# Attention and soft mixture of experts on one core: the output in three column groups instead of two halves, with a new order of stores and weight loads

## The chip, the core and the metric

The program runs on one core of a Trainium2 chip. The core has a matrix engine (PE, whose weight loads are shown apart as PEld), a vector engine (DVE), a scalar engine (ACT), GpSimd (POOL) and a sync engine (SP). In this kernel SP issues every transfer between the chip's main memory (HBM) and the on-chip memory, and sixteen DMA engines carry them out. Matrix products land in PSUM, the PE's accumulator memory, from which DVE or ACT copies a result to the on-chip memory.

The metric is the device time of one execution in microseconds (us). Before the change it is 398.29 us, the median of three runs (398.01 to 398.84).

## What is computed

Attention with a sigmoid in place of the softmax, for 8 batches of 12 heads, 448 tokens and 64 columns per head. Its output, as 3584 rows of 768 columns, goes through a soft mixture of 8 experts with 4 slots each:

```python
scores = scale * np.matmul(q, k.transpose(0, 1, 3, 2)) - np.log(S)
attn = 1.0 / (1.0 + np.exp(-scores))
x = (attn @ v)                                  # 3584 x 768
...
logits = x @ phi                                # 3584 x 32
d = softmax of logits over the rows;  slot_input = d.T @ x
for e in range(E):
    h = np.maximum(slot_input[e] @ w1[e], 0.0)  # 4 x 1024
    slot_out[e] = h @ w2[e]                     # 4 x 768
c = softmax of logits over the columns
return c @ slot_out                             # 3584 x 768
```

The weights are large beside the work: `w1` and `w2` hold 25.2 MB each, and the output 11.0 MB, all in float32.

## The kernel before

The program has three stages. The first is the attention, up to about 290 us, in which the rows of `x`, the logits and the running slot inputs are made. The second multiplies the slot inputs by `w1` (`w1_part`, line 518, and `h_part`, line 535), expert by expert, up to about 327 us. The third, which the change is about, multiplies by `w2` and makes the output.

Weights come in units: 128 partitions of 768 float32 columns, 384 KB, 3072 bytes to a partition, 64 units for `w1` and then 64 for `w2`. `load_unit` (line 92) puts the next unit into the next slot of a ring of 68 (`wa0` to `wa48`, `wb0` to `wb18`) and has SP issue its DMA. Output tiles take slots of the same ring in turn. SP runs its DMAs strictly in the order of the program, and a DMA whose slot or data is not ready holds all behind it. 49 units are loaded in the course of the attention, 19 right after it, and the others in `load_more`, two at a time, which stops `N_LATE` = 16 units before the end.

The third stage computes the output in two halves of 384 columns. For a half, sixteen steps (`w2_step`, line 583, one for each expert and each half of its 1024 hidden columns) accumulate into one PSUM tile, `po`; a step has four matmuls, side by side in four column groups of the array, and reads two units. `gather` (line 589) copies `po` to the on-chip memory, `sum_groups` (lines 594 and 596) adds the four partial sums with one matmul and a copy, giving `st`. Then `out_batch` (lines 561 and 566) multiplies `st` by the combine weights of one batch, four matmuls into two `px` tiles of a pool of three, and copies the two tiles out, one on ACT (128 partitions) and one on DVE (96 partitions). Each copy becomes one store, so that a batch has a pair of stores (line 574), of 384 KB and 288 KB.

The second half's steps and the first half's output are interwoven. After step 1 of the second half comes `sum_groups` of the first, and from step 3 on each step is followed by one `out_batch` of the first half. With each of the first four of these (`N_MIX`) the program puts the pair of stores and four of the 16 late units into SP's queue. After each of the steps 10 to 13 it adds three matmuls whose result is not used (`warm`, line 578). After the last step come the stores of the first half that are left, then `sum_groups` of the second half and its eight batches with their stores:

```python
    for i in range(2 * E):
        w2_step(po, 1, *divmod(i, 2))
        if i == 1:
            st = sum_groups(so)
        if 3 <= i < 3 + B:
            out_batch(0, i - 3, st)
            if i < 3 + N_MIX:
                store(2)
                for _ in range(N_LATE // N_MIX):
                    load_unit()
```

Of the kernel before, what the change touches and what calls it, by code (L numbers as in the profile page):

```python
# [9 lines left out]
F32 = mybir.dt.float32  # L10
# [6 lines left out]
B, H, S, D = 8, 12, 448, 64  # L17
DM, NSLOT, E, SPE, F = 768, 32, 8, 4, 1024
P = 128
# [3 lines left out]
NQ = NPR // 2  # L23
NKC = DM // P
NFC = F // P
HALF = DM // 2
UNIT = 768
N_A = 49
N_B = 19
N_LATE = 16  # L30
N_MIX = 4
NATT = 5
QW = 2 * S
NP = B * NPR
# [6 lines left out]
TOK = (128, 128, 96, 96)  # L41
# [6 lines left out]
def soft_moe_attention(ctx: ExitStack, tc: tile.TileContext, qk, v, phi, w1, w2, cst, out):  # L48
    nc = tc.nc
# [7 lines left out]
    ident = csb[:, 0:128]  # L57
    rep = csb[:, 128:256]
# [4 lines left out]
    lt_all = cpool.tile([P, B, P], F32, name="lt_all")  # L63
# [6 lines left out]
    nc.gpsimd.memset(lt_all, NEG)  # L70

    units = [("w1", e, 2 * uu + y, kh) for e in range(E) for uu in range(2) for kh in range(2) for y in range(2)]
    units += [("w2", hf, e, g, y) for hf in range(2) for e in range(E) for g in range(2) for y in range(2)]
    state = {"next": 0, "ring": 0, "wpb": None}
    utile = {}

    def ring_tile(dt=F32):
        n = state["ring"]
        state["ring"] = n + 1
        n %= N_A + N_B  # L80
        if n < N_A:
            return wpa.tile([P, UNIT], dt, name=f"wa{n}")
        return state["wpb"].tile([P, UNIT], dt, name=f"wb{n - N_A}")

    def load_unit():
        n = state["next"]
        if n >= len(units):
            return
        state["next"] = n + 1
        u = units[n]  # L90
        t = ring_tile()[:]
        nc.sync.dma_start(t, w1[u[1:]] if u[0] == "w1" else w2[u[1:]])
        utile[u] = t
# [22 lines left out]
    with ExitStack() as actx:  # L116
# [216 lines left out]
        def last_job(b, lg):  # L333
# [153 lines left out]
    sb2 = ctx.enter_context(tc.tile_pool(name="sb2", bufs=1, reuse_waits="tile"))  # L487
    hT = []
# [11 lines left out]
    ps_o = ctx.enter_context(tc.tile_pool(name="ps_o", bufs=2, space=PSUM, reuse_waits="tile"))  # L500

    def px_tile():
        return ps_x.tile([P, 2, 512], F32, name="px")

    def load_more():
        if state["next"] < len(units) - N_LATE:
            load_unit()

    for _ in range(N_B):
# [2 lines left out]
    def w1_part(e):  # L512
        ph = px_tile()
        for uu in range(2):
            for k2 in range(NKC // 2):
                for j in range(4):
                    kh, kc = divmod(2 * k2 + j % 2, 3)
                    nc.tensor.matmul(  # L518
                        ph[32 * j:32 * j + 32, uu, 0:256], sT[:, 3 * kh + kc, :],
                        utile[("w1", e, 2 * uu + j // 2, kh)][:, kc * 256:(kc + 1) * 256],  # L520
                        start=(k2 == 0), stop=(k2 == NKC // 2 - 1))
# [32 lines left out]
            combine_d(B - 1, sb2.tile([P, P], F32, name="tmp")[:])  # L554
    h_part(*prev)

    def out_batch(hf, b, st):
        pf = [px_tile() for _ in range(2)]
        for j in range(4):
            r = slice(32 * j, 32 * j + 32)  # L560
            nc.tensor.matmul(  # L561
                pf[j // 2][0:TOK[j], j % 2, 0:HALF], lt_all[r, b, 0:TOK[j]], st[r, :], start=True, stop=True)
        for g in range(2):
            n = TOK[2 * g]
            ov = ring_tile()[0:n, :].rearrange("p (j c) -> p j c", j=2)
            (nc.scalar.copy if g == 0 else nc.vector.tensor_copy)(ov, pf[g][0:n, :, 0:HALF])  # L566
            r0 = b * S + TOF[2 * g]
            stores.append((out[r0:r0 + 2 * n, hf * HALF:(hf + 1) * HALF].rearrange("(j p) c -> p j c", p=n), ov))

    stores = deque()  # L570

    def store(n):
        for _ in range(min(n, len(stores))):
            nc.sync.dma_start(*stores.popleft())

    def warm(n):
        for _ in range(n):
            nc.tensor.matmul(wt[:, 0:P], ident, ident, start=True, stop=True)

    def w2_step(po, hf, e, g):  # L580
        for fl in range(4):
            ut = utile[("w2", hf, e, g, fl // 2)][:, fl % 2 * HALF:(fl % 2 + 1) * HALF]
            nc.tensor.matmul(  # L583
                po[32 * fl:32 * fl + 32, 0:HALF], hT[e][:, 4 * g + fl, :], ut,
                start=(e == 0 and g == 0), stop=(e == E - 1 and g == 1))

    def gather(po):
        so = sb2.tile([P, HALF], F32, name="tmp")
        nc.scalar.copy(so[:], po[:, 0:HALF])
        return so  # L590

    def sum_groups(so):
        pr = px_tile()[:, 0, :]
        nc.tensor.matmul(pr[:, 0:HALF], rep, so[:], start=True, stop=True)
        st = sb2.tile([P, HALF], F32, name="st", bufs=2)
        nc.vector.tensor_copy(st[:], pr[:, 0:HALF])  # L596
        return st

    po = ps_o.tile([P, 512], F32, name="po")
    for e in range(E):  # L600
        for g in range(2):
            w2_step(po, 0, e, g)
            load_more()
            load_more()
    so = gather(po)
    po = ps_o.tile([P, 512], F32, name="po")
    wt = ps_o.tile([P, 512], F32, name="po")
    for i in range(2 * E):
        w2_step(po, 1, *divmod(i, 2))
        if i == 1:  # L610
            st = sum_groups(so)
        if 3 <= i < 3 + B:
            out_batch(0, i - 3, st)
            if i < 3 + N_MIX:
                store(2)
                for _ in range(N_LATE // N_MIX):
                    load_unit()
        if 2 + B <= i < 2 * E - 2:
            warm(3)
    so = gather(po)  # L620
    store(len(stores))
    st = sum_groups(so)
    for b in range(B):
        out_batch(1, b, st)
        store(2)


# [33 lines left out]
```

## Time and profile before

| quantity | value |
|---|---|
| median of three runs | 398.29 us |
| the profiled execution: its own time | 401.23 us |
| its span, first to last instruction | 399.5 us |
| PE busy | 371.3 us (93%) |
| DVE busy | 228.7 us (57%) |
| ACT busy | 186.1 us (47%) |
| weights, inputs and output moved | 97.52 MB, 244 GB/s over the span |
| mean granted PE clock | 0.98 |

The share of busy time says little here, since the stages have different limits: in the attention the PE is busy without a break, and in the last hundred microseconds the DMA engines are. A stretch of the span has therefore to be read by itself, its DMA rate beside its engines' busy time. Times within the span are counted from its start.

### The profile page before, as it was taken

The numbers are of one execution on the slowest core, as the hardware profiler recorded it, in microseconds if no ns is written. First come the engines' busy times: TensorE is split into PE (matmuls) and PEld (weight loads), VectorE is DVE, ScalarE is ACT, GpSimd is POOL, SyncE is SP. The second block draws the span as 40 slices with busy tenths as digits, with TensorE's granted clock in tenths as the row PEclk, the third lists the DMA queues.
The fourth block names the chain that finished last, engine by engine and source line by source line (L and its number), as shares of the span: only waits on it lengthen the run. The fifth ranks groups of instructions, "written<-read, shape, count | busy, mean of one in ns | idle before, by whom it ended". The sixth has DMA issues, their size and how long they took to land.

```text
span 399.5 us, 9562 instructions
## 1 busy us (share of the span) xinstructions
PE 371.3 (93%) x4000; PEld 195.1 (49%) x4000; DVE 228.7 (57%) x531; ACT 186.1 (47%) x244; POOL 3.4 (1%) x13
## 2 busy tenths in 40 slices
PE   8999999999999999899999999999989989978740
PEld 6555455555545555365545556555465543223210
DVE  3566668668777766765677777677532420330340
ACT  5655666662566656265625666564530110220330
POOL 1000000000000000000000000000010000000000
PEclk9999999999999999989999999999999999999985
DMA  7556567645655755475546656632899999999996
GB/s 237 197 189 232 180 235 257 222 150 161 225 199 192 276 199 178 140 250 178 180 120 251 220 175 239 235 126 71 304 344 334 405 400 400 400 410 409 355 288 205
DMA packets 41851, 97.52 MB, mean 244 GB/s; under 512 B 4304, under 2 KB 16208, under 8 KB 41808
## 3 DMA queue, kind: packets, MB, share of 16 engines
q1 hardware_dynamic: 41808, 96.91, 69.1%
q8 instruction: 31, 0.51, 0.5%
q14 instruction: 12, 0.10, 0.1%
HBM read 85.43 MB, written 11.47 MB: 243 GB/s over the span
## 4 chain that ended last, share of the span: by engine, by line
PE 78%; DMA 12%; DVE 3%; issue 2%; SPq 1%; ACT 0%; ACTq 0%
PE b L186 25%; PE b L168 21%; PE b L195 6%; PE px L518 5%; PE b L307 4%; PE po L583 4%; PE b L179 4%; DMA wb<-in_w_dram 4%; DMA zd<-t 3%; PE b L215 3%; PE px L561 2%; DMA dr<-zd 2%; DMA wa<-in_w_dram 2%; DMA out_dram<-wa 1%; PE px L535 1%
## 5 line engine op out<-in xcount | busy, mean ns | idle before, releaser
L158 ACT ACTIVATE att<-b,nbias 128x896 f32<-128x896 f32 x144 | 132.1, 1020 | 1.3 <-PE b L168 1.1
L186 PE MATMUL b<-att,v 128*64 128x448 f32 x576 | 115.3, 545 | 0.1
L168 PE MATMUL b<-qs,ks 64*128 64x448 f32 x864 | 96.3, 373 | 0.7 <-issue 0.5
L168 PEld LDWEIGHTS b<-qs,ks 64*128 64x128 f32 x864 | 80.2, 188 | 24.8 <-PE b L195 14.8
L186 PEld LDWEIGHTS b<-att,v 128*64 128x64 f32 x576 | 38.5, 137 | 62.6 <-issue 47.4
L158 ACT ACTIVATE attm<-b,nbias 128x896 f32<-128x896 f32 x24 | 24.2, 1010 | 71.6 <-PE b L179 71.6
L147 DVE CAST qs<-qkt 128x448 fp32r<-128x448 f32 x48 | 18.8, 392 | 51.5 <-DMA qkt<-in_qk_dram 47.4
L149 DVE TENSOR_TENSOR qs<-qkt,qs 128x448 fp32r<-128x448 f32 x48 | 30.0, 626 | 1.6
L204 DVE COPY xT<-b 128x896 f32<-128x896 f32 x23 | 25.1, 1090 | 8.6 <-PE b L195 8.5
L149 DVE TENSOR_TENSOR ks<-qkt,ks 128x384 fp32r<-128x384 f32 x48 | 26.8, 558 | 1.6
L210 DVE STREAM_TRANSPOSE y<-xT 128x448 f32<-128x448 f32 x48 | 27.3, 618 | 0.4
L179 PE MATMUL b<-qkt 64*64 64x448 f32 x192 | 22.9, 538 | 2.2 <-issue 2.2
L195 PE MATMUL b<-attm,v 64*64 64x448 f32 x192 | 23.6, 562 | 0.0
L307 PE MATMUL b<-y,dr 32*32 32x192 f32 x896 | 20.0, 332 | 0.8 <-DMA dr<-zd 0.5
L566 DVE COPY wa<-px 96x768 f32<-96x768 f32 x13 | 12.2, 952 | 13.5 <-PE px L561 12.7
L518 PE MATMUL px<-wa,sT 128*32 128x256 f32 x294 | 17.8, 381 | 0.9 <-DVE sT L378 0.9
L566 ACT COPY wa<-px 128x768 f32<-128x768 f32 x13 | 10.3, 799 | 17.9 <-PE px L561 15.2
L561 PE MATMUL px<-st,lt_all 32*128 32x384 f32 (+1 forms) x128 | 16.7, 525 | 1.5 <-DVE st L596 0.7
L215 PEld LDWEIGHTS b<-xT,phit 128*32 128x32 f32 x384 | 9.1, 109 | 17.0 <-issue 11.3
L147 DVE CAST ks<-qkt 128x384 fp32r<-128x384 f32 x47 | 16.6, 353 | 0.0
L215 PE MATMUL b<-xT,phit 128*32 128x96 f32 (+1 forms) x384 | 16.0, 266 | 0.2
L307 PEld LDWEIGHTS b<-y,dr 32*32 32x32 f32 x896 | 12.8, 103 | 6.5 <-DMA dr<-zd 2.3
(132 smaller groups left out, 223.4 us busy)
## 6 DMA issues: line engine op xcount, KB each, us to landing
wa<-in_w_dram SPq DMA_DIRECT2D x96, 384.0 KB, 7.7
qkt<-in_qk_dram SPq DMA_DIRECT2D x48, 448.0 KB, 5.0
wb<-in_w_dram SPq DMA_DIRECT2D x32, 384.0 KB, 7.1
v<-in_v_dram SPq DMA_DIRECT2D x24, 448.0 KB, 3.3
out_dram<-wa SPq DMA_DIRECT2D x13, 384.0 KB, 5.8
out_dram<-wa SPq DMA_DIRECT2D x13, 288.0 KB, 5.6
dr<-zd SPq DMA_DIRECT2D x28, 64.0 KB, 2.0
out_dram<-wb SPq DMA_DIRECT2D x3, 384.0 KB, 7.3
```

The costliest lines, as they stand in the source:

```text
L147: copy(dst[:, 0, :], src)
L149: nc.vector.tensor_tensor(out=dst[:, 1, :], in0=src, in1=dst[:, 0, :].bitcast(F32), op=ALU.subtract)
L158: nc.scalar.activation(att[:], sc[:, :, 0:S], AF.Sigmoid, bias=nbias, scale=QSCALE)
L168: nc.tensor.matmul(sc[:, h, 0:S], ks[r, z, c * P:(c + 1) * P], qs[r, y, :], start=(z + y == 0), stop=(z == 1))
L179: nc.tensor.matmul(sc[r, h, 0:S], t[d, S + NQK:QW], t[d, 0:S], start=True, stop=True)
L186: nc.tensor.matmul(avs["p", p][r, 0:S], vs[n][:, i * (NFULL + 1) + c, r], atts[p, c][:, h, :], start=(start and c == 0), stop=(stop and c ...
L195: nc.tensor.matmul(avs["p", 2 * n + i][d, 0:S], vt[r, NFULL, d], att[r, h, :], start=start, stop=stop)
L204: nc.vector.tensor_copy(xTs[n][:], avs[n][:, :, 0:S])
L210: nc.vector.transpose(ys[b][:, hp, :], xTs["p", p])
L215: nc.tensor.matmul(lp[32 * j:32 * j + 32, 0:TOK[j]], phi_sb[:, p % NPR, :], xTs["p", p][:, TOF[j]:TOF[j] + TOK[j]], start=(first and m == ...
L307: nc.tensor.matmul(sl[a // 2][32 * j:32 * j + 32, a % 2, 0:NPR * BLK], drs[b][32 * a:32 * a + 32, j, c * BLK:(c + 1) * BLK], y[32 * a:32 * ...
L518: nc.tensor.matmul(ph[32 * j:32 * j + 32, uu, 0:256], sT[:, 3 * kh + kc, :], utile[("w1", e, 2 * uu + j // 2, kh)][:, kc * 256:(kc + 1) * ...
```

## The change

The output is made in three column groups of 256. A step of 256 columns reads four pieces of 256 columns, and a unit holds three such pieces, so that the 64 units of `w2` are cut anew on the host, in the order of the steps: a group takes 64 pieces, 21 1/3 units. The steps number 48 instead of 32, `gather` and `sum_groups` run three times instead of twice, and 24 `out_batch` calls instead of 16 make 48 stores of 256 KB and 192 KB instead of 32 of 384 KB and 288 KB. A row of a store goes from 1536 to 1024 bytes. The `warm` matmuls are gone.

32 units instead of 16 are now late. 16 of them stand in pairs behind the eight pairs of stores of the first group; the other 16 behind the first five pairs of the second group, as 4, 3, 3, 3 and 3.

```diff
+NCG = 3
+CG = DM // NCG
-N_LATE = 16
-N_MIX = 4
+LATE = ((2,) * B, (4, 3, 3, 3, 3))
...
     def load_more():
-        if state["next"] < len(units) - N_LATE:
+        if state["next"] < len(units) - sum(LATE[0] + LATE[1]):
             load_unit()
...
-    def w2_step(po, hf, e, g):
+    def w2_step(po, cg, e, g):
         for fl in range(4):
-            ut = utile[("w2", hf, e, g, fl // 2)][:, fl % 2 * HALF:(fl % 2 + 1) * HALF]
+            u, y = divmod((cg * E + e) * NFC + 4 * g + fl, 3)
             nc.tensor.matmul(
-                po[32 * fl:32 * fl + 32, 0:HALF], hT[e][:, 4 * g + fl, :], ut,
+                po[32 * fl:32 * fl + 32, 0:CG], hT[e][:, 4 * g + fl, :], utile["w2", u][:, y * CG:(y + 1) * CG],
                 start=(e == 0 and g == 0), stop=(e == E - 1 and g == 1))
...
+    for cg in range(NCG):
+        po = ps_o.tile([P, 512], F32, name="po")
+        for i in range(2 * E):
+            w2_step(po, cg, *divmod(i, 2))
+            if cg == 0:
+                load_more()
+                load_more()
+                continue
+            if i == 1:
+                st = sum_groups(so)
+            if 3 <= i < 3 + B:
+                b = i - 3
+                out_batch(cg - 1, b, st)
+                if b < len(LATE[cg - 1]):
+                    store(2)
+                    for _ in range(LATE[cg - 1][b]):
+                        load_unit()
+        so = gather(po)
     store(len(stores))
     st = sum_groups(so)
     for b in range(B):
-        out_batch(1, b, st)
+        out_batch(NCG - 1, b, st)
         store(2)
```

The first place is SP's queue where the first stores come. Before, the last units of `load_more` and then the first pair; the names are ring slots:

```order
L92 DMA wa38_3998<-in_w2_dram 128x768
L92 DMA wa39_4000<-in_w2_dram 128x768
L92 DMA wa40_4023<-in_w2_dram 128x768
L92 DMA wa41_4025<-in_w2_dram 128x768
L92 DMA wa42_4031<-in_w2_dram 128x768
L92 DMA wa43_4033<-in_w2_dram 128x768
L574 DMA out_0_dram<-wa44_4240 128x2x384
```

The same place in SP's queue after the change:

```order
L92 DMA wa26_3918<-in_w2_dram 128x768
L92 DMA wa27_3920<-in_w2_dram 128x768
L574 DMA out_0_dram<-wa28_4207 128x2x256
L574 DMA out_0_dram<-wa29_4209 96x2x256
L92 DMA wa30_4213<-in_w2_dram 128x768
L92 DMA wa31_4215<-in_w2_dram 128x768
L574 DMA out_0_dram<-wa32_4227 128x2x256
L574 DMA out_0_dram<-wa33_4229 96x2x256
```

The last load ahead of the first store is now that of slot 27 and no longer that of slot 43: sixteen loads that stood ahead of the first store stand behind it.

The second place is SP's queue where the stores of the first group end and those of the second begin, after the change (slots `wb9` and `wb10` hold the last two units of the first sixteen late ones):

```order
L574 DMA out_0_dram<-wb7_4347 128x2x256
L574 DMA out_0_dram<-wb8_4349 96x2x256
L92 DMA wb9_4353<-in_w2_dram 128x768
L92 DMA wb10_4355<-in_w2_dram 128x768
L574 DMA out_0_dram<-wb11_4406 128x2x256
L574 DMA out_0_dram<-wb12_4408 96x2x256
L92 DMA wb13_4412<-in_w2_dram 128x768
L92 DMA wb14_4414<-in_w2_dram 128x768
L92 DMA wb15_4416<-in_w2_dram 128x768
L92 DMA wb16_4418<-in_w2_dram 128x768
L574 DMA out_0_dram<-wb17_4430 128x2x256
```

And the PE at the same place, after the change (`px` is the tile of an `out_batch`, `po` that of the third group):

```order
L590 MATMUL px_4388<-tmp_4377,csb_66 128x256
L579 MATMUL po_4379<-wb6_4335,acc_3694 32x256 x2
L579 MATMUL po_4379<-wb9_4353,acc_3694 32x256 x3
L579 MATMUL po_4379<-wb10_4355,acc_3694 32x256 x3
L561 MATMUL px_4400<-st_4390,lt_all_70 128x256 x2
L561 MATMUL px_4401<-st_4390,lt_all_70 96x256 x2
L579 MATMUL po_4379<-wb13_4412,acc_3694 32x256 x3
L579 MATMUL po_4379<-wb14_4414,acc_3694 32x256
L561 MATMUL px_4424<-st_4390,lt_all_70 128x256 x2
L561 MATMUL px_4425<-st_4390,lt_all_70 96x256 x2
```

The pair in `wb11` and `wb12` is the copy of the first two `px` tiles here. On the PE these stand behind the matmuls that read `wb10`, and in SP's queue the load of `wb10` is the last transfer ahead of that pair. Before the change there was no second group, and the last loads and the first half's last four pairs followed each other in SP's queue without such a border.

More of the change, by code (lines that the diff above doesn't have):

```diff
@@ L25 @@
 NFC = F // P
-HALF = DM // 2
+NCG = 3
+CG = DM // NCG
 UNIT = 768
@@ L72, in soft_moe_attention @@
     units = [("w1", e, 2 * uu + y, kh) for e in range(E) for uu in range(2) for kh in range(2) for y in range(2)]
-    units += [("w2", hf, e, g, y) for hf in range(2) for e in range(E) for g in range(2) for y in range(2)]
+    units += [("w2", i) for i in range(NCG * E * NFC // 3)]
     state = {"next": 0, "ring": 0, "wpb": None}
@@ L555, in soft_moe_attention, with out_batch @@
     h_part(*prev)
-    def out_batch(hf, b, st):
+    def out_batch(cg, b, st):
         pf = [px_tile() for _ in range(2)]
@@ L561, in out_batch @@
             nc.tensor.matmul(
-                pf[j // 2][0:TOK[j], j % 2, 0:HALF], lt_all[r, b, 0:TOK[j]], st[r, :], start=True, stop=True)
+                pf[j // 2][0:TOK[j], j % 2, 0:CG], lt_all[r, b, 0:TOK[j]], st[r, :], start=True, stop=True)
         for g in range(2):
             n = TOK[2 * g]
-            ov = ring_tile()[0:n, :].rearrange("p (j c) -> p j c", j=2)
-            (nc.scalar.copy if g == 0 else nc.vector.tensor_copy)(ov, pf[g][0:n, :, 0:HALF])
+            ov = ring_tile()[0:n, 0:2 * CG].rearrange("p (j c) -> p j c", j=2)
+            (nc.scalar.copy if g == 0 else nc.vector.tensor_copy)(ov, pf[g][0:n, :, 0:CG])
             r0 = b * S + TOF[2 * g]
-            stores.append((out[r0:r0 + 2 * n, hf * HALF:(hf + 1) * HALF].rearrange("(j p) c -> p j c", p=n), ov))
+            stores.append((out[r0:r0 + 2 * n, cg * CG:(cg + 1) * CG].rearrange("(j p) c -> p j c", p=n), ov))
     stores = deque()
@@ L574, in store @@
             nc.sync.dma_start(*stores.popleft())
-    def warm(n):
-        for _ in range(n):
-            nc.tensor.matmul(wt[:, 0:P], ident, ident, start=True, stop=True)
-    def w2_step(po, hf, e, g):
+    def w2_step(po, cg, e, g):
         for fl in range(4):
-            ut = utile[("w2", hf, e, g, fl // 2)][:, fl % 2 * HALF:(fl % 2 + 1) * HALF]
+            u, y = divmod((cg * E + e) * NFC + 4 * g + fl, 3)
             nc.tensor.matmul(
-                po[32 * fl:32 * fl + 32, 0:HALF], hT[e][:, 4 * g + fl, :], ut,
+                po[32 * fl:32 * fl + 32, 0:CG], hT[e][:, 4 * g + fl, :], utile["w2", u][:, y * CG:(y + 1) * CG],
                 start=(e == 0 and g == 0), stop=(e == E - 1 and g == 1))
     def gather(po):
-        so = sb2.tile([P, HALF], F32, name="tmp")
-        nc.scalar.copy(so[:], po[:, 0:HALF])
+        so = sb2.tile([P, CG], F32, name="tmp")
+        nc.scalar.copy(so[:], po[:, 0:CG])
         return so
@@ L593, in sum_groups @@
         pr = px_tile()[:, 0, :]
-        nc.tensor.matmul(pr[:, 0:HALF], rep, so[:], start=True, stop=True)
-        st = sb2.tile([P, HALF], F32, name="st", bufs=2)
-        nc.vector.tensor_copy(st[:], pr[:, 0:HALF])
-        return st
[L599 to L620, printed above, removed]
+        nc.tensor.matmul(pr[:, 0:CG], rep, so[:], start=True, stop=True)
+        st = sb2.tile([P, CG], F32, name="st", bufs=2)
+        nc.vector.tensor_copy(st[:], pr[:, 0:CG])
+        return st
+    for cg in range(NCG):
[16 more added lines that the diff above has]
+        so = gather(po)
     store(len(stores))
@@ L642 @@
     w1 = inputs["moe_w1"].reshape(E, 2, 3, P, 4, 256).transpose(0, 4, 1, 3, 2, 5).reshape(E, 4, 2, P, UNIT)
-    w2 = inputs["moe_w2"].reshape(E, 2, 2, 2, P, 2, HALF).transpose(5, 0, 1, 3, 4, 2, 6).reshape(2, E, 2, 2, P, UNIT)
+    w2 = inputs["moe_w2"].reshape(E, 2, 2, 2, P, NCG, CG).transpose(5, 0, 1, 3, 2, 4, 6).reshape(-1, 3, P, CG)
+    w2 = w2.transpose(0, 2, 1, 3).reshape(-1, P, UNIT)
     cst = np.zeros((P, CW), np.float32)
```

## Prediction

> **What bounds the kernel now.** I read the chain of work that ended last first, then the rates by stretch, then the packets. The chain, where the third stage runs (start, duration, what):
>
> ```profile
> 345.43 7.49 DMA wa<-in_w_dram
> ...
> 356.53 7.32 DMA wb<-in_w_dram
> ...
> 363.92 7.35 DMA wb<-in_w_dram
> ```
>
> The chain goes through transfers, and the PE only takes what has landed. The stretches show it (PE, PEld, DVE, ACT and POOL busy, then the granted PE clock, the DMA engines' share and GB/s):
>
> ```profile
> 310.00:330.00 20.00, 18.79 (x284) 10.23 (x280) 6.73 (x19) 2.80 (x13) 0.00 (x0) 1.00 1.03 402
> ...
> 350.00:360.00 10.00, 7.85 (x58) 2.07 (x56) 3.08 (x4) 2.40 (x3) 0.00 (x0) 1.00 1.04 410
> 360.00:372.00 12.00, 10.27 (x68) 4.29 (x64) 0.95 (x1) 0.80 (x1) 0.00 (x0) 1.00 1.04 407
> 372.00:374.00 2.00, 1.06 (x4) 0.30 (x2) 0.27 (x1) 0.48 (x1) 0.00 (x0) 1.00 1.07 401
> ...
> 378.00:398.00 20.00, 6.20 (x40) 2.28 (x40) 5.58 (x7) 4.12 (x6) 0.00 (x0) 0.71 0.85 264
> ```
>
> From 310 to 374 us the sixteen engines are full (a share over 1, since packets overlap a little) at 401 to 410 GB/s, loads and stores alike. After 374 us only stores are left, and the rate falls to 264. So from about 310 us on the end is set by bytes over rate, plus any time in which the queue stands empty; before the change it never does until the last half's stores. What the change can win is the slow stretch: fewer bytes left for it. What it can lose is a hole in the queue, and at 400 GB/s no later stretch can make up for one.
>
> Packets of three stretches (310 to 330, 372 to 374 and 386 to 394 us), each with the share of the queue's packets in sixteen engines' time:
>
> ```profile
> q1 hardware_dynamic: 2930, 8.00, 102.4%
> ```
>
> ```profile
> q1 hardware_dynamic: 560, 0.80, 107.2%
> ```
>
> ```profile
> q1 hardware_dynamic: 1589, 2.28, 93.0%
> ```
>
> 8.00 MB of loads are 2604 packets of 3072 bytes (the rest are small marks): 1.024 x 16 x 20 / 2604 = 0.1258 us each. 0.80 MB of stores are 522 packets of 1536 bytes: 1.072 x 16 x 2 / 522 = 0.0657. In the third stretch 2.28 MB in 8 us are 286 GB/s.
>
> **The first hole.** SP's queue around the last loads ahead of the stores (start, duration):
>
> ```profile
> 325.76 0.33 SPq L92 DMA_DIRECT2D wa<-in_w_dram  x1
> ```
>
> ```profile
> 341.36 0.33 SPq L92 DMA_DIRECT2D wa<-in_w_dram  x1
> 343.90 0.90 SPq L574 DMA_DIRECT2D out_dram<-wa  x2
> ```
>
> ```profile
> v<-in_v_dram SPq DMA_DIRECT2D x24, 448.0 KB, 3.3
> ...
> wa<-in_w_dram SPq DMA_DIRECT2D x47, 384.0 KB, 7.7
> ```
>
> A load takes 0.393 MB / 0.405 = 0.97 us of the engines and 7.7 us from issue to landing, so eight are under way. Before, the last early load is issued at 341.36 and the first store 2.5 us later: the queue stays fed. The change withholds 16 more loads; counted back at 0.97 us apiece, the last early one is the load issued at 325.76, which lands at 325.76 + 7.7 = 333.5. Behind it SP holds the first store, for which group 0 has to be finished. PE, ACT and DVE rows for that:
>
> ```profile
> 305.58 2.80 PE L518 MATMUL px<-wa,sT 128*32 128x256 f32 x48
> ...
> 327.36 1.50 PE L583 MATMUL po<-wb,acc 128*32 128x384 f32 x16
> ...
> 339.11 0.91 PE L594 MATMUL px<-tmp,csb 128*128 128x384 f32 x2
> ```
>
> ```profile
> L566 DVE COPY wa<-px 96x768 f32<-96x768 f32 x8 | 7.4, 950 | 3.8 <-PE px L561 3.0 <-DMA out_dram<-wa 0.8
> ...
> L561 PE MATMUL px<-st,lt_all 32*128 32x384 f32 x32 | 7.0, 527 | 1.2 <-DVE st L596 0.7 <-DVE wa L566 0.5
> ...
> L566 ACT COPY wa<-px 128x768 f32<-128x768 f32 x8 | 6.3, 799 | 5.5 <-PE px L561 2.8 <-DMA out_dram<-wa 2.6
> ...
> L596 DVE COPY st<-px 128x384 f32<-128x384 f32 x1 | 0.6, 558 | 12.6 <-PE px L594 12.6
> L589 ACT COPY tmp<-po 128x384 f32<-128x384 f32 x1 | 0.5, 478 | 11.3 <-PE po L583 11.3
> ```
>
> A step of 256 columns has the form of line 518's matmuls (128x256 on 32 columns): 24 matmuls, six rounds of four, in 2.73 us to the next line's start, 0.455 us a step. Group 0 needs nothing but early units, so it runs from 327.36 for 16 x 0.455 = 7.3, to 334.66. Two steps of the next group (0.91, the `gather` beside them), `sum_groups` at two thirds of 0.91 less its overlap, 0.57, two more steps (0.91, the copy to `st`, 0.43, beside them), half of an `out_batch` (0.30) and ACT's copy: from 0.478 us for 384 and 0.799 for 768 elements it takes 0.59 for 512. Together 334.66 + 0.91 + 0.57 + 0.91 + 0.30 + 0.59 = 337.9, rounded to 338.0 with the waits between engines. A transfer that finds the queue empty lands its own time plus about 2.1 us after issue (3.3 us for 448 KB of `v`, of which 1.13 are transfer). So the landings resume as from 340.1 instead of 333.5: **6.6 us** without data.
>
> **The second and third hole.** Group 0's stores then run well: steps 4 to 7 need early units only, SP refills up to eight transfers, and eight pairs (1.22 us each, below) and 16 loads (0.97) take 25.3 us, until about 365. But the load in `wb10` is the last in the queue, and the next pair needs the step that reads it. Behind its landing come a step 0.46, half an `out_batch` 0.30, ACT 0.59, waits 0.05 and the 2.1 of an empty queue: 3.5 us. The step after that needs the second of the next four loads (`wb14`), behind which two loads are under way (1.94 us): another 3.5 - 1.94 = 1.5 us. From then on the loads run ahead.
>
> The clock raises both. Rows of a stretch in the attention, where the PE waited:
>
> ```profile
> 168.00:171.00 3.00, 0.83 (x13) 0.20 (x7) 3.00 (x7) 0.00 (x0) 0.00 (x0) 1.00 0.49 156
> 171.00:175.00 4.00, 4.00 (x28) 3.17 (x22) 2.11 (x4) 2.92 (x3) 0.00 (x0) 0.57 0.56 150
> ```
>
> After three microseconds with the PE 28% busy it ran for most of the next four at half clock. Between its landings the changed kernel's PE has a step and at times an `out_batch` (0.46 + 0.60) in 3.1 us, a pair and two loads: 34% busy and less, and the `warm` matmuls, which fill such waits before the change, are gone. At half clock step and half `out_batch` cost 0.76 more: holes of **4.3 and 2.3 us**. I take that. (The Trainium skill, "TensorE: Matmul & The Clock Gate", What's actually happening, has the clock fall only after a wholly idle window of about 3.4 us; by that rule a PE that does a step in every load's time keeps its full clock, and this is a rival below. The rows above, a fall after 2.2 us of waiting, speak against it.)
>
> **The last group.** Behind the last load stand three pairs of the second group, 3 x 1.22 = 3.7 us. Meanwhile the last step (0.46), `gather` 0.37, `sum_groups` 0.57, `st` 0.43, half an `out_batch` 0.30, the copy 0.59, waits 0.1 and 2.1: 4.9 us at full clock, 6.3 at half. The difference, **1.2 us** (2.6 at half clock), is a fourth hole. I take the full clock here, since the last three or four loads come without stores between them.
>
> **Packets.** No row has a packet of 1024 bytes. From the two above, 0.0391 us per 1000 bytes and 0.0056 fixed: 0.0457, an estimate. A pair then takes 28 packets an engine, 1.28 us, 1.22 with the overlap of about 5%; at 405 GB/s it would take 1.13. Ends: nothing (by bytes) and 0.0657 a packet, the 1536-byte row (0.62 a pair more). I take the estimate, 0.09 x 16 pairs ahead of the last group, less what 1536-byte stores already lose: **+1.0 us**, between 0 and +9. (By the Trainium skill, "Advanced Engine Details and Errata", Clock Domains, an unobstructed 1 KiB descriptor takes 42 to 43 ns, by which a pair would be near 1.15 us and this term +0.3.)
>
> **What it wins.** The slow stretch holds 3.67 MB instead of 5.51. At its 286 GB/s that is 12.8 us instead of 19.3, and the 1.84 MB moved ahead cost 4.5 at 405: **-1.9 us**. Here too there are two ends: if each packet, not each byte, takes the time, 3584 packets of 1024 bytes need the same 19.3 us, and the term is +4.5. At full rate (401) it would be -5.6. I take bytes; the loads above were bound by bytes at both packet sizes.
>
> **The sum.** 6.6 + 4.3 + 2.3 + 1.2 + 1.0 - 1.9 = **+13.5 us**. Copies (48 of 0.59 and 0.69 us instead of 32 of 0.80 and 0.95), the third `gather` and `sum_groups` and the PE's steps cost nothing beyond this: the PE has waits for landings beside them; without that cover the third `sum_groups` with its copies would be 1.4 us. The profiled span of 399.5 would become 413.0, its execution's 401.23 us 414.7; the median lies 2.9 below that execution, so 398.3 + 13.5 = **411.8**.
>
> **Rivals.**
> Faster: the holes stay covered. It takes the first pair ready by 331.4 us (333.5 less 2.1). Then 8.26 MB behind the last load become 5.05; before, they took from 371.3 (the last load of the chain, 363.92 + 7.35) to about 398.4, 304 GB/s; 5.05 MB take 16.6 instead of 27.1 and the moved 3.2 MB 7.9: -2.6, 395.7 us. For it: the rate in mixed stretches, 407 against 264. Against it: at 331.4 the PE would have done about 9 of the 16 steps of group 0. It decides once all holes together are under 2.6 us. Chance 0.05; another 0.03 that holes and gain cancel.
> Full clock throughout: 6.6 + 3.5 + 1.5 + 1.2 + 1.0 - 1.9 = +11.9, 410.2. Half clock also at the end: +14.9, 413.2. These belong to the forecast's family, 0.62 together.
> The slow stretch is bound by packets: +4.5 for -1.9, 418.2. For it: the drop in rate comes with stores alone. Against it: stores alone went at 401 from 372 to 374. Chance 0.15.
> Smaller holes, if an empty queue answers sooner or group 0 is faster than line 518: 403 to 408, chance 0.12. More than all this, 0.03.
>
> **Range.** 406 to 419 leaves out about 2 in 10. A measurement of this kernel tells about 0.2% from no change; slower by more than that 0.92, within it 0.03, faster 0.05.
>
> **What would show it.** In the changed profile: a stretch of several microseconds near 334 to 340 us with hardly any bytes and SP waiting for ACT's copy; two smaller ones near 365 and 373; a granted clock of 0.5 in parts of 345 to 390; the last load landing near 390 instead of 371; some 13 us of stores alone after it at 250 to 290 GB/s. I am wrong if SP issues the first store before 333 us, if the rate in the mixed stretch is far from 400, or if the stores alone run at 400.

## The result, and the profile after

The changed kernel takes **421.88 us**, the median of five runs (420.04 to 422.49); the kernel before, on the same chip, 398.44 us (398.01 to 398.89). The ratio is **1.0579**, with a 95% interval from 1.0552 to 1.0606: slower by 23.4 us. The forecast was slower, 411.8 us with a range up to 419.0. The direction held and the size did not: the time lies 10.1 us above the forecast and outside its range. The profiled execution of the changed kernel took 422.49 us with a span of 420.7, where before it was 401.23 and 399.5. Some executions of a kernel on this chip fall into a slower state; the ratios here and below leave them out and the medians keep them (so that a ratio need not be the quotient of two medians), and one trace, that of the kernel with many warm matmuls, is of such an execution.

The GB/s in the page's slices of the changed kernel (40 slices of 10.5 us; the third stage begins in the 32nd):

```profile
GB/s 230 176 203 227 199 178 245 207 158 253 215 201 164 218 192 219 219 219 151 193 242 195 164 245 132 150 165 320 315 404 400 224 235 401 315 193 272 400 190 246
```

Before, the rate stood at about 400 or more from 310 to 374 us. Now it falls in three places, to 224, 193 and 190 GB/s, with slices at 400 between them. The same by stretches of 5 us (PE, PEld, DVE, ACT and POOL busy, granted PE clock, DMA share, GB/s):

```profile
330.00:335.00 5.00, 5.00 (x100) 2.99 (x92) 0.00 (x0) 0.37 (x1) 0.00 (x0) 1.00 0.41 156
335.00:340.00 5.00, 5.00 (x66) 2.06 (x58) 1.80 (x3) 1.17 (x2) 0.00 (x0) 1.00 0.17 54
340.00:345.00 5.00, 3.39 (x42) 1.19 (x38) 2.06 (x3) 1.75 (x3) 0.00 (x0) 1.00 0.91 276
...
360.00:365.00 5.00, 3.12 (x19) 0.73 (x20) 0.00 (x0) 0.37 (x1) 0.00 (x0) 0.50 1.06 405
365.00:370.00 5.00, 4.75 (x29) 1.60 (x27) 0.56 (x2) 0.20 (x1) 0.00 (x0) 0.58 0.18 70
370.00:375.00 5.00, 0.00 (x0) 0.00 (x0) 0.55 (x1) 0.39 (x1) 0.00 (x0) 0.76 0.72 210
375.00:380.00 5.00, 4.55 (x32) 1.38 (x32) 0.69 (x1) 0.58 (x1) 0.00 (x0) 0.55 0.49 196
380.00:385.00 5.00, 2.06 (x30) 0.74 (x22) 1.37 (x2) 1.17 (x2) 0.00 (x0) 1.00 0.94 257
385.00:390.00 5.00, 4.36 (x37) 1.50 (x34) 0.82 (x2) 0.78 (x2) 0.00 (x0) 0.66 1.03 385
...
400.00:405.00 5.00, 3.68 (x20) 1.69 (x15) 0.67 (x2) 0.68 (x2) 0.00 (x0) 0.50 0.44 153
405.00:410.00 5.00, 5.00 (x36) 2.74 (x32) 2.50 (x4) 2.62 (x5) 0.00 (x0) 0.50 0.73 213
```

What each stretch loses against a full queue is 5 us x (1 - rate / 405). 330 to 345 lose 3.1 + 4.3 + 1.6 = 9.0 us, 365 to 390 lose 4.1 + 2.4 + 2.6 + 1.8 + 0.2 = 11.2, and 400 to 405 lose 3.1. In the stretches between, at 395 to 405 GB/s, next to nothing is lost. SP's queue shows why the bytes stop (start, duration, what; "x2" is a pair):

```profile
320.33 6.14 SPq L92 DMA_DIRECT2D wa<-in_w_dram  x7
338.30 1.19 SPq L574 DMA_DIRECT2D out_dram<-wa  x2
...
370.42 0.91 SPq L574 DMA_DIRECT2D out_dram<-wb  x2
371.41 1.87 SPq L92 DMA_DIRECT2D wb<-in_w_dram  x4
379.27 0.92 SPq L574 DMA_DIRECT2D out_dram<-wb  x2
...
405.30 11.52 SPq L574 DMA_DIRECT2D out_dram<-wa  x16
```

The last early load is issued at 326.1 and lands at 334.0 by the trace's transfer records; SP's next DMA is the first store, 4.3 us after that. The same happens before the stores at 370.42, 379.27 and 405.30: each is issued after the last transfer ahead of it has landed (at 367.88, 378.24 and 403.37). What SP waited for, over the third stage (us in total, times, longest us):

```profile
SPq L574 <- ACT wa L566: 20.3, 7, 11.2
SPq L574 <- ACT wb L566: 14.5, 3, 7.9
```

The same wait before the change:

```profile
SPq L574 <- ACT wa L566: 6.8, 4, 3.0
```

The chain that ended last now leaves the transfers at 399.80 (393.05 + 6.75) and ends on the PE and its copies:

```profile
371.41 4.00 DMA wb<-in_w_dram
...
375.45 2.00 PE po L579 x8
377.46 1.16 PE px L561 x6
...
393.05 6.75 DMA wa<-in_w_dram
...
399.85 1.06 PE po L579 x6
...
401.26 0.38 ACT tmp L585
...
401.69 1.23 PE px L590 x2
...
402.94 0.43 DVE st L592
...
403.42 10.84 PE px L561 x62
```

Before, the chain went from load to load up to 371.26 with the queue full. Here it also runs through steps and batches of the PE, and at 399.85 through five links before the first store of the last group can go.

### The profile page after: what moved, and what is told of

Read it like the earlier page. It is cut to its first block, busy times and chain, and to the rows that moved or that the text cites. A ratio compares the mean times of both kernels' runs of the same rounds, so it can differ in the third digit from the quotient of the medians.

```text
span 420.7 us, 9955 instructions
## 1 busy us (share of the span) xinstructions
PE 384.6 (91%) x4170; PEld 200.4 (48%) x4170; DVE 230.1 (55%) x540; ACT 187.0 (44%) x253; POOL 3.4 (1%) x13
## 4 chain that ended last, share of the span: by engine, by line
PE 82%; DMA 12%; DVE 1%; issue 1%; SPq 1%; ACT 1%; ACTq 0%
PE b L186 26%; PE b L168 21%; DMA wa<-in_w_dram 6%; PE b L195 5%; PE px L518 5%; PE po L579 5%; PE px L561 4%; PE b L179 4%; PE b L307 4%; PE b L215 3%; DMA wb<-in_w_dram 3%; DMA zd<-t 1%; PE px L535 1%; DMA v<-in_v_dram 1%; PE b L402 1%
## 5 line engine op out<-in xcount | busy, mean ns | idle before, releaser
L168 PEld LDWEIGHTS b<-qs,ks 64*128 64x128 f32 x864 | 78.5, 185 | 26.4 <-PE b L195 15.5
L561 PE MATMUL px<-st,lt_all 32*128 32x256 f32 (+1 forms) x192 | 25.0, 553 | 0.5 <-DVE st L592 0.5
L179 PE MATMUL b<-qkt 64*64 64x448 f32 x192 | 23.8, 555 | 1.9 <-issue 1.9
L566 ACT COPY wa<-px 128x512 f32<-128x512 f32 x20 | 11.7, 585 | 28.4 <-PE px L561 27.8
L566 DVE COPY wa<-px 96x512 f32<-96x512 f32 x19 | 13.0, 687 | 20.1 <-PE px L561 20.1
L579 PE MATMUL po<-wa,h 128*32 128x256 f32 x140 | 14.1, 417 | 6.9 <-DMA wa<-in_w_dram 6.9
L592 DVE COPY st<-px 128x256 f32<-128x256 f32 x3 | 1.3, 424 | 32.7 <-PE px L590 32.7
L561 PEld LDWEIGHTS px<-st,lt_all 32*128 32x128 f32 (+1 forms) x192 | 12.1, 228 | 14.5 <-issue 6.2
```

The source lines that it names most:

```text
L168: nc.tensor.matmul(sc[:, h, 0:S], ks[r, z, c * P:(c + 1) * P], qs[r, y, :], start=(z + y == 0), stop=(z == 1))
L179: nc.tensor.matmul(sc[r, h, 0:S], t[d, S + NQK:QW], t[d, 0:S], start=True, stop=True)
L561: nc.tensor.matmul(pf[j // 2][0:TOK[j], j % 2, 0:CG], lt_all[r, b, 0:TOK[j]], st[r, :], start=True, stop=True)
L579: nc.tensor.matmul(po[32 * fl:32 * fl + 32, 0:CG], hT[e][:, 4 * g + fl, :], utile["w2", u][:, y * CG:(y + 1) * CG], start=(e == 0 and g == ...
```

## The experiments

The theory after the result: the loss is the emptying of SP's queue, and an emptying costs more than the wait and a transfer's start, since the rate comes back slowly. The rivals: the smaller and more numerous stores and copies; the half clock; and the slow rate of stores alone. All edits are to the changed kernel unless the heading names the kernel before. The times scatter by about 2% between runs, most of it ahead of the third stage, whose first step starts between 326.1 and 334.2 us in the traces, so the table gives beside the ratio (to the kernel before on the same chip) four times of each trace, by its transfer records.

| kernel | late units | last early load landed | first store issued | last load landed | last store landed | ratio, 95% interval |
|---|---|---|---|---|---|---|
| before | 16 | 349.30 | 343.90 | 371.26 | 398.43 | 1 |
| the change | 32 | 334.00 | 338.30 | 399.80 | 419.70 | 1.0579 (1.0552 to 1.0606) |
| late in group 1 only | 16 | 348.60 | 341.90 | 373.19 | 396.36 | 1.0042 (0.9998 to 1.0087) |
| late in group 2 only | 16 | 347.73 | 340.94 | 385.50 | 405.01 | 1.0236 (1.0178 to 1.0294) |
| halves, 24 late | 24 | 343.55 | 346.14 | 384.14 | 409.73 | 1.0325 (1.0268 to 1.0383) |
| three groups, 24 late, fed | 24 | 343.25 | 340.00 | 381.45 | 401.70 | 1.0077 (1.0039 to 1.0115) |
| border fed | 32 | 337.97 | 344.19 | 398.16 | 416.94 | 1.0419 (1.0304 to 1.0533) |
| warm matmuls, many | 32 | 338.78 | 345.12 | 406.00 | 426.00 | 1.0612 (1.0499 to 1.0725) |
| warm matmuls, few | 32 | 334.26 | 339.66 | 400.58 | 420.04 | 1.0549 (1.0450 to 1.0647) |

### The 16 late units of the first group alone

```diff
-LATE = ((2,) * B, (4, 3, 3, 3, 3))
+LATE = ((2,) * B, ())
```

> Three column groups as changed, but only 16 late units, in pairs behind the first group's eight pairs of stores; none behind the second group's. Theory 'empty queue' (each time SP's queue runs empty costs the time until bytes land again, plus a refill at 250 to 280 GB/s): the queue never empties before the last group, since 112 units are issued ahead of the first store as before. Last load lands near 374 (32 loads of 0.97 and 8 pairs of 1.22 from 333.5), then 8 pairs 9.8, then the last group's 3.67 MB in 10 to 13 us: 394 to 398 us, faster than before. Theory 'smaller stores' (48 stores with 1024-byte rows and their copies are what costs): slower than before, 405 us or more. Theory 'clock' (the missing extra matmuls): some 3 us at the end only, 400 us.

Measured: 399.39 us, ratio 1.0042 (0.9998 to 1.0087), so no loss, but not the gain down to 394 to 398 us that was expected either. Three groups, rows of 1024 bytes, 48 stores and 48 copies are all in this kernel. Its stretches:

```profile
335.00:340.00 5.00, 5.00 (x72) 2.08 (x63) 2.24 (x4) 1.76 (x3) 0.00 (x0) 1.00 1.03 400
...
365.00:370.00 5.00, 2.66 (x26) 0.60 (x22) 0.69 (x1) 0.58 (x1) 0.00 (x0) 1.00 1.05 397
```

The first store is issued 6.7 us ahead of the last early landing, the share stays above 1 and the rate at 390 to 401 through the mixed stretch. Net of the shorter slow stretch, smaller stores and their copies thus cost 0.4% here, 0.9% at the interval's far end, and the rival that blames them for the 5.8% falls. What moving stores ahead wins at the end (23.2 us from the last load to the last store instead of 27.2) is mostly paid beforehand (the last load lands at 373.2 instead of 371.3).

### The 16 late units of the second group alone

```diff
-LATE = ((2,) * B, (4, 3, 3, 3, 3))
+LATE = ((0,) * B, (4, 3, 3, 3, 3))
```

> Three column groups, 16 late units, all behind the second group's first five pairs (4, 3, 3, 3, 3) as changed; none behind the first group's. The first and the second emptying of the queue are gone, the third (second pair of the second group) and the wait ahead of the last group stay. Theory 'empty queue': 16 loads and 8 pairs from 333.5 to 359, five pairs and 16 loads to 380, one emptying of about 4, last load at 384, the last group as in the changed kernel: 401 to 406 us. Theory 'smaller stores': still above 415 us.

Measured: 407.6 us, ratio 1.0236 (1.0178 to 1.0294). This is a little more than the 401 to 406 expected. The first hole is gone (first store 6.8 us ahead of the last early landing); the one ahead of the second group's second pair stands (this pair is issued at 364.11, 0.8 us after the last landing), with stretches of 177 GB/s (360 to 365 us) and 270 (365 to 370). Neither set of 16 late units alone costs what the two together cost (1.0042 and 1.0236 against 1.0579): only with both does the first store have no load under way ahead of it.

### The kernel before, with 24 late units

```diff
-N_LATE = 16
+N_LATE = 24
```

> The kernel before with 24 late units instead of 16 (six behind each of the first four pairs), nothing else. Its last early load lands near 341.3, the first store is issued near 343.9: the queue empties once. Theory 'empty queue': 4.7 us until bytes land again plus about 1.7 of refill, about +6.4: 404 to 406 us. Theory that only the groups' number matters: no change, 398 to 399 us.

Measured: 410.84 us, ratio 1.0325 (1.0268 to 1.0383). This kernel has the old halves, with rows of 1536 bytes. SP's queue, then its stretches:

```profile
346.14 0.91 SPq L574 DMA_DIRECT2D out_dram<-wa  x2
...
356.88 0.91 SPq L574 DMA_DIRECT2D out_dram<-wa  x2
```

```profile
340.00:345.00 5.00, 4.91 (x42) 1.31 (x34) 0.56 (x1) 0.48 (x1) 0.00 (x0) 1.00 0.42 162
345.00:350.00 5.00, 0.27 (x4) 0.00 (x0) 0.95 (x1) 0.80 (x1) 0.00 (x0) 0.73 0.57 170
350.00:355.00 5.00, 3.00 (x12) 0.88 (x16) 0.00 (x0) 0.00 (x0) 0.00 (x0) 0.50 0.98 350
355.00:360.00 5.00, 5.00 (x40) 1.15 (x32) 1.91 (x2) 1.60 (x2) 0.00 (x0) 0.75 0.67 214
360.00:365.00 5.00, 2.27 (x14) 0.75 (x16) 0.95 (x1) 0.80 (x1) 0.00 (x0) 0.94 1.00 330
```

The queue empties once and later runs down to a single transfer, and the kernel is slower with nothing of the three groups in it. The forecast of 404 to 406 us had only the first of these. The first emptying has a gap of 346.14 - 343.55 = 2.6 us and, with the 2.1 us of a transfer that finds the queue empty, should lose 4.7; the stretches from 340 to 355 lose 3.0 + 2.9 + 0.7 = 6.6. The second loses 2.4 + 0.9 = 3.3 where the wait accounts for 1.7 (the last landing is at 357.33, 0.45 us behind the issue). So each of the two costs 1.6 to 1.9 us beyond the wait and the start.

### The border between the groups fed

```diff
-LATE = ((2,) * B, (4, 3, 3, 3, 3))
+LATE = ((2, 2, 2, 2, 2, 2, 2, 6), (0, 3, 3, 3, 3))
```

> The changed kernel, with the four late units of the second group's first pair moved ahead of that pair (behind the first group's last pair: 6 instead of 2, then 0, 3, 3, 3, 3); nothing else. The first emptying (338 us) stays, the second and third should go, since 3.9 us of loads are under way while the PE, ACT and SP make the pair. Theory 'empty queue': of the 5.3 and 5.4 us lost at these two places about 8 come back: 412 to 415 us. Rival (the loss sits in packets, copies or the clock): 420 to 422.

Measured: 419.0 us, ratio 1.0419 (1.0304 to 1.0533): faster than the change, but not the 412 to 415 us expected. All 32 units are still late, but four loads of the second group stand ahead of its first pair. From the first store's issue to the last store's landing it takes 72.75 us, where the changed kernel takes 81.40: 8.65 less. The attention of this profiled execution ended 5.9 us later than that of the changed kernel (first step at 333.29 and 327.40), so the spans don't show it. The dip at the border is now one instead of two:

```profile
370.00:375.00 5.00, 5.00 (x37) 1.70 (x34) 0.64 (x2) 0.28 (x1) 0.00 (x0) 0.76 1.03 414
375.00:380.00 5.00, 4.05 (x48) 1.48 (x42) 2.53 (x4) 2.06 (x4) 0.00 (x0) 1.00 0.74 219
380.00:385.00 5.00, 1.84 (x8) 0.33 (x8) 0.00 (x0) 0.00 (x0) 0.00 (x0) 0.76 0.96 293
385.00:390.00 5.00, 5.00 (x41) 1.71 (x40) 1.37 (x2) 1.17 (x2) 0.00 (x0) 0.56 1.05 404
```

The queue never stood empty there: the next pair was issued at 375.33, 1.9 us before the last landing ahead of it. It ran down to two or three transfers, and that alone cost 2.3 + 1.4 = 3.7 us. The changed kernel loses 11.2 from 365 to 390, so that 7.5 of the 8.65 us come from the border.

### Three groups with 24 late units, fed ahead of the stores and at the border

```diff
-LATE = ((2,) * B, (4, 3, 3, 3, 3))
+LATE = ((2, 2, 2, 2, 2, 2, 2, 4), (0, 3, 3))
```

> The changed kernel with 24 late units: two behind each of the first group's first seven pairs, four behind the eighth, three behind the second and the third pair of the second group. Stores of both groups still stand between loads, but by the reckoning the queue never empties: the last early load lands near 341, the first pair is ready at 338.3, and at the border three or four loads are under way while the next pair is made. Theory 'empty queue': from the first store's issue to the end about 58 us as with 16 late units, instead of 81; 396 to 402 us. Rival (late units or stores between loads cost by themselves): 408 or more.

Measured: 402.91 us, ratio 1.0077 (1.0039 to 1.0115), with as many late units as the halves that took 1.0325.

```profile
340.00:345.00 5.00, 5.00 (x66) 1.97 (x66) 2.63 (x5) 2.25 (x4) 0.00 (x0) 1.00 0.97 311
345.00:350.00 5.00, 5.00 (x76) 2.51 (x76) 2.32 (x4) 1.86 (x4) 0.00 (x0) 1.00 1.00 340
...
365.00:370.00 5.00, 3.84 (x36) 1.29 (x38) 1.41 (x3) 1.17 (x2) 0.00 (x0) 1.00 1.04 407
...
385.00:390.00 5.00, 5.00 (x34) 3.04 (x36) 2.06 (x3) 1.77 (x4) 0.00 (x0) 0.50 0.69 215
```

The first store goes out 3.3 us ahead of the last early landing and the border is fed. What is left is a queue that has run down to four transfers at the first store (311 and 340 GB/s from 340 to 350, 2.0 us), and one that has run down to two ahead of the last group (215 GB/s, 2.3 us); from the first store to the end it takes 61.7 us, where 58 were expected. It is not the number of withheld loads that costs, but that the queue runs down.

### The clock restored

Unused matmuls in the waits of the second and third group's steps, many in the first kernel and few in the second:

```diff
+            if cg == 1 and i >= 8 or cg == 2 and i < 2 * E - 1:
+                warm(4)
```

```diff
+            if cg > 0 and 11 <= i < 2 * E - 1:
+                warm(2)
+            if cg == 2 and i == 3:
+                warm(8)
```

> The changed kernel with four extra matmuls of 128 columns after the steps in which the PE waits (steps 8 to 15 of the second group, 0 to 14 of the third), as before the change; their results are not used. Theory 'clock': the granted clock stays at 1.0 through the third stage, and the steps, sums and copies behind each emptying and the last group shorten: 415 to 418 us instead of 421.9. Theory 'empty queue' alone: the queue still empties at the same places; less than 1.5 us are won, 420.4 to 421.9.

> The changed kernel with extra matmuls only where the PE surely waits: two after each of steps 11 to 14 of the second and third groups, eight after step 3 of the third; their results are not used. Theory 'clock': the step behind the third emptying and the last group run at full clock, about 1 us at the third emptying, 1.4 us ahead of the last group's first store and up to 1 us in its copies: 418 to 420 us. Theory that the clock is beside the point: 421 to 423.

Measured: ratios 1.0612 (1.0499 to 1.0725) and 1.0549 (1.0450 to 1.0647), both as the change within their intervals, and neither faster than it, as the theory 'clock' had it. From first store to end they take 80.9 and 80.4 us, the change 81.4. With many, the clock stood at 1.00 in most stretches, but the matmuls themselves held up the steps: the last step ended 2.9 us after the last load instead of 1.1. With few, the first store of the last group followed the last load by 4.6 us instead of 5.5. The half clock is thus worth about 1 us as far as it could be taken away, and it is not the main cause. What a full clock without extra matmuls would save was not shown.

### The last stores: more of them ready, a second queue, a warm clock

Four kernels on why stores alone move slowly. The first is the kernel before with the last half's 16 stores held until all are ready, the second the kernel before with every first store of a last pair issued by ACT's queue; the third and the fourth are the kernel with late units in the first group only, once with warm matmuls and once with ACT's queue.

```diff
-            nc.sync.dma_start(*stores.popleft())
+            nc.sync.dma_start(*(stores.pop() if last else stores.popleft()))
...
-        store(2)
+    store(len(stores), last=True)
```

> The kernel before, with the last half's 16 stores issued in reverse order, so that SP waits for the last copy and then finds all 16 ready: eight under way at once. If the slow stretch of stores (264 to 286 GB/s) comes from too few stores under way, they now run at 380 to 400 GB/s: 5.5 MB in 14 us behind the last copy near 386, end near 402. If stores alone are slow by themselves, 19 us behind it: 407 or more.

```diff
-            nc.sync.dma_start(*stores.popleft())
+            (nc.scalar if both and k == 0 else nc.sync).dma_start(*stores.popleft())
...
-        store(2)
+        store(2, both=True)
```

> The kernel before; of the last half's stores the 128-partition ones are issued by ACT, the 96-partition ones by SP. If the slow stretch of stores alone (264 to 300 GB/s with four or five under way) comes from the way one queue issues them, the last 5.5 MB run at up to 400 GB/s and the end comes up to 5 us earlier: 393 to 396 us. If stores alone are slow for another reason, within 1 us of before.

```diff
+            if cg == 2 and 11 <= i < 2 * E - 1:
+                warm(2)
```

> Three groups, 16 late units behind the first group's pairs only, with two extra matmuls after each of steps 11 to 14 of the third group (results not used). If the slow stores at the end come from the last group being made at half clock (1.35 us a pair against 1.22 us that the DMA engines need), they run at 370 GB/s and the end comes 3 us earlier than without, about 396 us. If the slow rate has another cause, 398 to 400.

> Three groups with 16 late units behind the first group's pairs only, and the last group's 128-partition stores issued by ACT. If one queue's issue limits stores alone, 3 to 4 us earlier than without: 394 to 396; otherwise 398 to 400.

Measured: held until ready, 411.03 us, ratio 1.0227 (1.0121 to 1.0332); the 16 stores, issued from 387.9 on with no copy to wait for, still need 20.8 us for 5.51 MB. SP's queue, then the stretches:

```profile
387.90 16.78 SPq L574 DMA_DIRECT2D out_dram<-wa  x16
```

```profile
388.00:398.00 10.00, 0.00 (x0) 0.00 (x0) 0.00 (x0) 0.00 (x0) 0.00 (x0) 0.58 0.92 292
398.00:409.00 11.00, 0.00 (x0) 0.00 (x0) 0.00 (x0) 0.00 (x0) 0.00 (x0) 0.50 0.75 235
```

The eight stores under way that this kernel was made for did not come about. With all 16 ready, SP still took 16.78 / 16 = 1.05 us for each issue, where the pair of stores issued at 343.90 before the change took it 0.90 together, and by the transfer records three to five stores were under way at a time, as many as in the kernel before from 380 to 396 us. So it shows that waiting for copies is not what holds the stores back, and not what eight under way would do.

Two queues on the kernel before: ratio 1.0011 (0.9965 to 1.0056), 27.12 us from last load to end where the kernel before takes 27.17:

```profile
380.00:385.00 5.00, 3.88 (x28) 1.40 (x24) 2.71 (x3) 1.76 (x3) 0.00 (x0) 1.00 0.99 304
```

Warm matmuls with late units in the first group only: ratio 1.0036 (0.9983 to 1.0089). The clock is full up to 385 us and the stores are as slow:

```profile
380.00:385.00 5.00, 4.33 (x42) 2.21 (x40) 3.55 (x6) 3.18 (x6) 0.00 (x0) 1.00 0.97 301
385.00:390.00 5.00, 0.26 (x4) 0.00 (x0) 0.69 (x1) 0.13 (x1) 0.00 (x0) 0.77 0.98 302
```

Two queues on that kernel: ratio 0.9980 (0.9935 to 1.0025). Neither the readiness of the copies, nor the number of queues, nor the clock sets the rate of stores alone, and the bytes of a row make little difference: from 385 to 390 us the kernel with late units in the first group only, with 1024-byte rows, moves 297 GB/s, and the kernel before, with 1536-byte rows, 286 from 390 to 395. What does set it stays open; the number of transfers under way is a rival that no run varied by itself. No kernel of these can be told from the kernel before as faster.

## Why the prediction was wrong in size

**The first hole: place and wait right, price too low.** The first store was forecast for 338.0 and was issued at 338.30; the landing before it for 333.5, and it came at 334.0. The wait is 4.3 us, where 4.5 stood in the sum. The start was shorter than its 2.1 us: this store of 0.26 MB landed 2.30 us after its issue, and 0.65 of these are its own time at 405 GB/s. From landing to landing the hole is thus 6.0 us, not 6.6. But the stretches up to 345 lose 9.0 us, and 0.2 more up to 360, where the hole and the packets of eight pairs (0.7) were to cost 7.3. The step that failed is that the queue runs at full rate up to its last landing and resumes at full rate from the first new one: the sum has no term for the run-out and the refill, and here they are worth about 3 us. From 331 to 334 us, ahead of the last landing, the rate is 265, 95 and 12 GB/s in one microsecond after the other; from 339 to 343, with SP issuing again, it is 238. The transfers of 380 to 385 us show the refill, beside those of 350 to 360 (packets with how many are small, then the queue's share of sixteen engines' time):

```profile
DMA packets 776, 1.29 MB, mean 257 GB/s; under 512 B 59, under 2 KB 507, under 8 KB 776
...
q1 hardware_dynamic: 776, 1.29, 94.0%
```

```profile
DMA packets 2499, 4.00 MB, mean 400 GB/s; under 512 B 206, under 2 KB 1699, under 8 KB 2498
...
q1 hardware_dynamic: 2498, 3.98, 104.8%
```

With the prediction's 0.0457 us for a packet of 1024 bytes and 0.1258 for one of 3072, the second stretch should take 1493 x 0.0457 + 800 x 0.1258 = 168.9 us of engine time, and takes 1.048 x 160 = 167.7: the prediction's packet price was right for a full queue. The first should take 448 x 0.0457 + 269 x 0.1258 = 54.3, and takes 0.94 x 80 = 75.2. After an emptying the engines count as busy, and the packets take 1.38 times as long on average. This does not hold for every packet: by the trace's packet records the median is 46 ns for 1024 bytes and 121 ns for 3072 in both stretches. But from 380 to 385 us 145 of 717 packets take over 1.3 times their median, up to 1.6 us, and from 350 to 360 only 6 of 2292. Most packets are as fast as ever, and one in five stalls.

**The second and third hole: +11.2 instead of 6.6.** They stand where they were forecast in SP's queue, behind the load in `wb10` and behind the four loads after it, at half clock (0.58 and 0.55) as was assumed. Counted from landing to landing as in the prediction they are 4.1 and 2.6 us (2.5 and 1.0 of wait, then 1.5 and 1.6 of start), where 4.3 and 2.3 stood. So the waits were right, and the other 4.5 of the 11.2 us are run-out and refill again: 380 to 390 loses 2.0 us with SP already issuing. That the waits came out so close is in part luck. The start had been put too high, and half an `out_batch` too low: in the third hole the copy on ACT started only when the four matmuls of its batch were all but done, 1.16 us at half clock instead of 0.60.

**The last group: +4.0 instead of 1.2.** From the last landing, 399.80, to the first store it took 5.5 us where 2.8 stood in the sum (4.9 less the 2.1). The chain shows the links: at half clock the step took 1.06 instead of 0.46, `sum_groups` 1.23 instead of 0.57, and the batch and its copy from 403.42 to 405.27. I had taken the full clock here, since the last loads come without stores between; the row from 400 to 405 has 0.50. With the start, counted as 2.1 here and in the next paragraph, and less the 3.6 us in which the leftover pairs still moved, this hole is 4.0. The rival of half clock at the end was right as to the clock, and too low in price.

**Packets and slow stretch: right.** The 16 last stores take 405.30 to 419.70, 12.3 us behind the 2.1 of the start, for which the sum had 12.8; the rate goes by bytes, and the rival by which it goes by packets (418.2) came near the time for a reason that is not the one at work. The full-clock rival (410.2) and that of smaller holes fell with the rows above; the faster one needed the first pair by 331.4.

**From the span to the median.** The terms give 1.9 more for the first hole, 4.6 for the next two, 2.8 for the last and 0.5 less for the slow stretch: 8.8. The span rose by 21.2 instead of 13.5, so 7.7 had to be found. The rest of 1.1 lies in the kernel before: behind its last load it takes 27.2 us for 8.26 MB and loses 6.8 against 405 GB/s, where the sum had 19.3 - 13.6 = 5.7 for the slow stretch. A further 2.3 us is no matter of the kernel: I had put the median 2.9 us below the profiled execution, as it lay before, but that of the changed kernel lies 0.6 below.

What of this was shown: that the emptied queue is the cause, by the three kernels that keep it fed and by the halves that empty it; that the price of an emptying is more than wait and start, by two kernels with different rows. Why some packets stall after an emptying was not tried and stays open.

The clock is half again in stretches in which the PE is busy for a good part: 0.50 from 360 to 365 us, with 3.12 us of 5 busy. The Trainium skill, "TensorE: Matmul & The Clock Gate", What's actually happening, gives half the clock as the state after one or more idle windows of some 3.4 us. From 340 to 366 us the PE's longest wait for a load was 1.9 us:

```profile
PE po L579 <- DMA wb<-in_w_dram: 2.9, 2, 1.9
```

If an idle window is one without any matmul, as the prediction read it, the measurement decides against the rule here, as it did there.

## What to carry to other kernels

Where one queue issues loads and stores in program order, withholding loads behind stores cost nothing here as long as the first store was issued 5 us or more before the last load ahead of it had landed (with 3.3 us it cost 2.0); where that margin is negative, the kernel pays the gap, a transfer's start, and some 1.5 to 3 us more until the rate is back. Work the margin out at every border between groups, with whole batches and the clock that the PE will have there, and put a few loads ahead of the first store behind each border. Moving stores ahead of the end wins little where the engines are already full: the same bytes are paid a little earlier (with late units in the first group only, 4.0 us were won behind the last load, and the ratio is 1.0042).

## What was not expected of the hardware

After an emptying the engines' share is soon back at 0.91 to 0.95 while the rate is 257 to 276 GB/s, where a share of 1.04 to 1.06 moves 395 to 405; in the kernel with the border fed, whose queue only ran down to two or three transfers, the share is 0.96 and the rate 293. The share says that a packet is under way, not that it moves.

Stores alone hold some 260 to 310 GB/s in every kernel here, after a start at full rate behind loads. The packets look as they do after an emptying: before the change 282 of 1484 take over 1.3 times the median of 65 ns from 386 to 394 us, and 1 of 522 from 372 to 374, at 401 GB/s. In both slow cases fewer transfers are under way, on average 4 to 6 with stores alone against nearly 8 in the full stretches. But the rate does not follow their number closely: the kernel with the border fed had 6.8 under way from 380 to 385 us at 293 GB/s, and the kernel before 6.6 from 372 to 374 at 401. Whether the two have one cause stays open.

A second queue brought nothing. The Trainium skill, "DMA: Bandwidth & Descriptors", Issuing engines are not separate DMA queues, says that DMAs from all issuing engines run on the same sixteen DMA engines, so that issuing from several saves only issue time; the two kernels with two queues agree (1.0011 and 0.9980).
